# Transposing softmax probabilities as 4-byte words of two bf16 keys in a cached-attention kernel

## The chip, the cores and the metric

The kernel runs on one core of one Trainium2 chip. The metric is the device time of one execution in microseconds (us). Three runs of the kernel before took 1212.93, 1213.23 and 1215.47 us; the median is 1213.23 us. The five engines of the core that the text names are TensorE (PE in the profile, with PEld for its weight loads), VectorE (DVE), ScalarE (ACT), GpSimd (POOL) and SyncE (SP, which here only issues DMAs).

## The reference, cut to what matters

Two problems, A and B, of the same shape are computed one after the other and their outputs put side by side. All inputs are bf16.

```python
# per problem: B=16 batch elements, Sq=144 queries, D=448, H=16 heads, Sk=512 keys, Dh=256
q = (x @ wq).reshape(B, Sq, H, Dh).transpose(0, 2, 1, 3)
scores = jnp.einsum("bhqd,bhkd->bhqk", q, k_cache) * (Dh ** -0.5)
p = softmax(scores, axis=-1)
o = jnp.einsum("bhqk,bhkd->bhqd", p, v_cache)
out = o.transpose(0, 2, 1, 3).reshape(B, Sq, H * Dh) @ wo
# result: concatenate([out_A, out_B], axis=-1)
```

## The kernel before, in words

One head of one batch element is a *unit*; there are 512 units, 256 for each problem. Four consecutive units are a *group* (128 of them) and eight units are what one load of keys covers.

The 144 queries of a unit are split into 112 (part A, handled unit by unit) and 32 (part B, handled for four units together, so that they fill 128 partitions). For every unit the kernel does the following.

- Q (L314): eight matmuls of 144 columns project x onto the head and leave q transposed in PSUM. It is evacuated to `qt_sb` by VectorE (L326) or ScalarE (L330), scaled by 1/16.
- SA (L418): two matmuls of 512 columns give the scores of the 112 queries in one of the two banks `sa_ps`. VectorE takes the negated maximum (L429); ScalarE takes the exponential into `pa_sb` as bf16 and sums it (L440); VectorE inverts the sum (L450); GpSimd multiplies the row by it (L458).
- TA (L471): TensorE transposes the probabilities, in four transposes of 112 queries by 128 keys. The data are the weights of the matmul and the identity is the operand that streams. The keys of one transpose are every fourth key: `pa_sb` is read with a step of four elements, since the values lie in SBUF with four consecutive keys in one partition. The result goes as bf16 into the same bank of `sa_ps` that held the scores of this unit, and VectorE copies it to `pt_sb` (L481).
- PV (L504): eight matmuls of 144 columns, four chunks of keys for each half of the head dimension. The weights are the values and the streaming operand is P^T out of `pt_sb`. ScalarE evacuates the result to a ring buffer (L519, L521).
- OP (L542): output projection, pieces of two matmuls of 448 columns, as soon as 128 rows of a batch element's heads are complete. ScalarE evacuates it (L560), and GpSimd's queue stores it (L571).

Part B goes the same way for groups: SB (L342) makes the scores of eight units with 16 matmuls that use 32 columns of weights each, TB (L394) makes four transposes of 128 by 128 for a group, and VectorE copies them to the four `pt_sb` slots of the group (L403). The softmax steps are L354, L364, L374 and L382.

The order of the work is written out as one loop over i. In iteration i the kernel emits Q of unit i+15, SB once in eight iterations, SA of unit i+5, TA of unit i+2, TB for a group once in four iterations, PV of unit i, and pieces of OP. Each engine executes its own list in that order. A small planner (`_Sched`) adds the waits: an operation waits on the semaphore counters of those that wrote what it reads, or that still use a buffer or a PSUM bank that it writes. PSUM banks are the scarce buffers: `sa_ps` has two, so the transposes of unit u+2 go into a bank that the scores of unit u+4 have just left, which means after the maximum and the exponential of unit u+4. SP's queue carries the loads of x, wq, wo, K (with a transposing DMA, L290, three buffers of eight units) and V (L299, three buffers of four units), in the order of planned due times.

`S.add(engine, emit, reads, writes, banks)` below records one operation for the planner; `pta_ps` and `ptb_ps` are the banks of part A and B as the transposes see them, before the change the bf16 view of the fp32 banks.

Of the kernel before, what the change touches and what calls it, by code (L numbers as in the profile page):

```python
# [5 lines left out]
BF16 = mybir.dt.bfloat16  # L6
F32 = mybir.dt.float32
# [115 lines left out]
def bass_concat_heads__mha_block_cached__gqa_block_cached__near_ridge_kernel(  # L123
# [19 lines left out]
    Bn, SQ, D = A_x.shape  # L143
# [3 lines left out]
    QA, QB = 112, 32  # L147
# [17 lines left out]
    NQT, NPA, NPB, NPT, NST, NSTB, NOST = 12, 5, 2, 8, 4, 2, 3  # L165
# [9 lines left out]
    with contextlib.ExitStack() as es:  # L175
        def sb(name, shape, dt):
            return es.enter_context(nc.sbuf_tensor(name, shape, dt))

        def ps(name, shape, dt):
            return es.enter_context(nc.psum_tensor(name, shape, dt))  # L180
# [7 lines left out]
        qt_sb = sb("qt_sb", [128, NQT, 2, SQ], BF16)  # L188
        pa_sb = sb("pa_sb", [128, NPA, SK], BF16)
        pb_sb = sb("pb_sb", [128, NPB, SK], BF16)  # L190
        pt_sb = sb("pt_sb", [128, NPT, 4, SQ], BF16)
        ost_sb = sb("ost_sb", [128, NOST, D], BF16)
        ident = sb("ident", [128, 128], BF16)
        ones = sb("ones", [128, 128], BF16)
        stat = sb("stat", [128, 3 * NST + 3 * NSTB + 2], F32)
        qp_ps = ps("qp_ps", [128, 512], F32)
        sa_ps = [ps("sa_ps%d" % i, [128, 512], F32) for i in range(2)]
        sb_ps = [ps("sb_ps%d" % i, [128, 512], F32) for i in range(2)]
        ot_ps = [ps("ot_ps%d" % i, [128, 512], F32) for i in range(2)]
        op_ps = ps("op_ps", [128, 512], F32)  # L200
        pta_ps = [t.bitcast(BF16) for t in sa_ps]
        ptb_ps = [t.bitcast(BF16) for t in sb_ps]

        S = _Sched()
        sem_names = list(COMPUTE)
# [181 lines left out]
        def t_tb(G):  # L387
            psl = G % NPB

            def e(t):  # L390
                src = pb_sb[:, psl, :].rearrange("q (p c) -> q c p", c=4)
                ins = None
                for c in range(4):
                    ins = t.transpose(ptb_ps[G % 2][:, c * 128:(c + 1) * 128], src[:, c, :], ident[:, :])  # L394
                return ins
            S.add(PE, e, reads=[(("pb", psl), (G, 1)), ("ident", 0)], writes=[(("sbb", G % 2), ("t", G))],
                  banks=["sb%d" % (G % 2)], name="TB%d" % G)

        def t_evac_ptb(G):
            s0 = (4 * G) % NPT  # L400

            def e(v):
                return v.tensor_copy(pt_sb[:, s0:s0 + 4, :, QA:SQ],  # L403
                                     ptb_ps[G % 2][:, 0:512].rearrange("p (c j q) -> p j c q", c=4, j=4))
            S.add(DVE, e, reads=[(("sbb", G % 2), ("t", G))],
                  writes=[(("ptb", (4 * G + j) % NPT), 4 * G + j) for j in range(4)], banks=["sb%d" % (G % 2)],
                  name="eptb%d" % G)
# [55 lines left out]
        def t_ta(U):  # L463
            psl = U % NPA
            bank = U % 2

            def e(t):
                src = pa_sb[0:QA, psl, :].rearrange("q (p c) -> q c p", c=4)
                ins = None
                for c in range(4):  # L470
                    ins = t.transpose(pta_ps[bank][:, c * 128:c * 128 + QA], src[:, c, :], ident[0:QA, 0:QA])  # L471
                return ins
            S.add(PE, e, reads=[(("pa", psl), (U, 1)), ("ident", 0)], writes=[(("sap", bank), ("t", U))],
                  banks=["sa%d" % bank], name="TA%d" % U)

        def t_evac_pta(U):
            sl = U % NPT
            bank = U % 2

            def e(v):  # L480
                return v.tensor_copy(pt_sb[:, sl, :, 0:QA],  # L481
                                     pta_ps[bank][:, 0:512].rearrange("p (c q) -> p c q", c=4)[:, :, 0:QA])
            S.add(DVE, e, reads=[(("sap", bank), ("t", U))], writes=[(("pta", sl), U)], banks=["sa%d" % bank],
                  name="epta%d" % U)

# [8 lines left out]
        def t_pv(U):  # L494
            G, j = divmod(U, 4)
            vsl = G % NV
            sl = U % NPT
            ob = U % 2

            def e(t):  # L500
                ins = None
                for dc in range(2):
                    for c in range(4):
                        ins = t.matmul(ot_ps[ob][:, dc * SQ:(dc + 1) * SQ],  # L504
                                       lhsT=v_sb[:, vsl, j, c * DH + dc * 128:c * DH + (dc + 1) * 128],
                                       rhs=pt_sb[:, sl, c, :], start=(c == 0), stop=(c == 3))
                return ins
            S.add(PE, e, reads=[(("v", vsl), G), (("pta", sl), U), (("ptb", sl), U)], writes=[(("otp", ob), U)],
                  banks=["ot%d" % ob], name="PV%d" % U)
# [75 lines left out]
        for XG in range(NXGT):  # L585
            pr, j = divmod(XG, Bn // XB)
# [214 lines left out]
```

## Time and profile before

| what | value |
|---|---|
| median of the runs | 1213.23 us (1212.93 to 1215.47) |
| profiled execution, first to last instruction | 1210.9 us |
| TensorE busy | 1176.6 us (97%), 13952 matmuls and as many weight loads |
| VectorE, ScalarE, GpSimd busy | 770.1, 753.9 and 679.6 us |
| granted TensorE clock, mean | 0.997 |
| transposes L471, L394 | 2048 and 512 matmuls |
| PV matmuls L504 | 4096 |
| HBM read and written | 148.90 MB and 4.13 MB |

How to read it: the span goes from the first to the last instruction of the profiled execution. No time of its own is listed for that execution beside its span; the span lies 2.3 us under the median of the runs. "Busy" counts the time in which at least one instruction of the engine was running; a matmul's duration includes its latency, and consecutive matmuls overlap. The chain is the sequence of work that ended last, followed back from the last instruction; its pieces add up to the span. A group of instructions shows line, engine, operation, out<-in, shapes and count, then busy time and mean ns of one, then the idle time of the engine just before them and who ended it.

### The profile page before, as it was taken

The numbers are of one execution on the slowest core, as the hardware profiler recorded it, in microseconds if no ns is written. First come the engines' busy times: TensorE is split into PE (matmuls) and PEld (weight loads), VectorE is DVE, ScalarE is ACT, GpSimd is POOL, SyncE is SP. The second block draws the span as 40 slices with busy tenths as digits, with TensorE's granted clock in tenths as the row PEclk, the third lists the DMA queues.
The fourth block names the chain that finished last, engine by engine and source line by source line (L and its number), as shares of the span: only waits on it lengthen the run. The fifth ranks groups of instructions, "written<-read, shape, count | busy, mean of one in ns | idle before, by whom it ended". The sixth has DMA issues, their size and how long they took to land.

```text
span 1210.9 us, 33868 instructions
## 1 busy us (share of the span) xinstructions
PE 1176.6 (97%) x13952; PEld 902.6 (75%) x13952; DVE 770.1 (64%) x2179; ACT 753.9 (62%) x2213; POOL 679.6 (56%) x682
## 2 busy tenths in 40 slices
PE   4998999999999999999999999999999999999997
PEld 3676777777777777777777777777877777777765
DVE  1765666666666666666566666666666666666563
ACT  1655666666666666666566666666666666666553
POOL 0654565565555565565555655655655655655553
PEclk9999999999999999999999999999999999999999
DMA  9999999999999999999999999999999999999971
GB/s 250 296 269 290 246 255 225 242 251 246 245 238 234 228 263 231 239 239 233 278 284 272 278 272 267 247 257 224 245 245 236 226 245 244 244 239 243 223 178 47
DMA packets 627033, 294.15 MB, mean 243 GB/s; under 512 B 548416, under 2 KB 556608, under 8 KB 626880
## 3 DMA queue, kind: packets, MB, share of 16 engines
q1 hardware_dynamic: 625152, 287.85, 102.2%
q0 software_dynamic: 1728, 4.13, 1.2%
q8 instruction: 111, 1.82, 0.6%
q14 instruction: 42, 0.34, 0.1%
HBM read 148.90 MB, written 4.13 MB: 126 GB/s over the span
## 4 chain that ended last, share of the span: by engine, by line
PE 90%; DMA 6%; DVE 2%; SPq 1%; ACT 0%; issue 0%; POOL 0%; ACTq 0%
PE qp_ps L314 20%; PE ot_ps L504 19%; PE sa_ps L418 18%; PE op_ps L542 17%; PE sa_ps L471 8%; PE sb_ps L342 5%; DMA kt_sb<-in_A_k_cache_dram 4%; PE sb_ps L394 2%; DMA kt_sb<-in_B_k_cache_dram 1%; DVE stat L429 1%; DMA wq_sb<-in_A_wq_dram 0%; PE qp_ps L542 0%; SPq L280 0%; DVE qt_sb L326 0%; DVE pt_sb L481 0%
## 5 line engine op out<-in xcount | busy, mean ns | idle before, releaser
L458 POOL TENSOR_TENSOR pa_sb<-pa_sb,stat 112x512 bf16<-112x512 bf16 x512 | 532.7, 1041 | 491.6 <-DVE stat L450 491.4
L440 ACT ACTIVATE pa_sb<-sa_ps,stat 112x512 bf16<-112x512 f32 x512 | 352.0, 688 | 409.6 <-DVE stat L429 408.6
L429 DVE TENSOR_REDUCE stat<-sa_ps 112x1 f32<-112x512 f32 x512 | 353.9, 691 | 324.7 <-PE sa_ps L418 321.4
L314 PEld LDWEIGHTS qp_ps<-xt_sb,wq_sb 128*128 128x128 bf16 x4096 | 290.5, 99 | 93.1 <-issue 11.3
L314 PE MATMUL qp_ps<-xt_sb,wq_sb 128*128 128x144 bf16 x4096 | 344.1, 228 | 16.1 <-DMA wq_sb<-in_A_wq_dram 10.3
L504 PE MATMUL ot_ps<-pt_sb,v_sb 128*128 128x144 bf16 x4096 | 340.9, 226 | 0.0
L418 PE MATMUL sa_ps<-kt_sb,qt_sb 128*112 128x512 bf16 x1024 | 311.1, 385 | 1.0 <-DVE pt_sb L481 0.8
L542 PE MATMUL op_ps<-wo_sb,ring 128*128 128x448 bf16 x1120 | 279.6, 353 | 0.0
L504 PEld LDWEIGHTS ot_ps<-pt_sb,v_sb 128*128 128x128 bf16 x4096 | 269.1, 98 | 0.4
L471 PEld LDWEIGHTS sa_ps<-ident,pa_sb 112*128 112x128 bf16 x2048 | 161.2, 114 | 104.9 <-ACT pa_sb L440 24.8
L519 ACT ACTIVATE ring<-ot_ps 128x288 bf16<-128x288 f32 (+8 forms) x512 | 190.3, 372 | 4.5 <-PE ot_ps L504 4.5
L481 DVE COPY pt_sb<-sa_ps 128x448 bf16<-128x448 bf16 x512 | 190.5, 372 | 2.4 <-PE sa_ps L471 2.4
L471 PE MATMUL sa_ps<-ident,pa_sb 112*128 112x112 bf16 x2048 | 186.5, 213 | 0.1
L326 DVE TENSOR_SCALAR qt_sb<-qp_ps 128x288 bf16<-128x288 f32 x256 | 117.0, 457 | 98.2 <-PE qp_ps L314 97.5
L382 POOL TENSOR_TENSOR pb_sb<-pb_sb,stat 128x512 bf16<-128x512 bf16 x128 | 133.1, 1040 | 27.1 <-DVE stat L374 27.1
L330 ACT ACTIVATE qt_sb<-qp_ps 128x288 bf16<-128x288 f32 x256 | 106.0, 414 | 35.1 <-PE qp_ps L314 33.4
L418 PEld LDWEIGHTS sa_ps<-kt_sb,qt_sb 128*112 128x112 bf16 x1024 | 96.9, 129 | 38.5 <-issue 26.8
L542 PEld LDWEIGHTS op_ps<-wo_sb,ring 128*128 128x128 bf16 x1120 | 95.5, 98 | 28.1 <-issue 0.9
L440 ACT ACTIVATION_READ_ACCUMULATOR pa_sb<-sa_ps,stat 112x1 f32 x512 | 98.9, 193 | 0.0
L354 DVE TENSOR_REDUCE stat<-sb_ps 128x1 f32<-128x512 f32 x128 | 87.1, 680 | 3.6 <-PE sb_ps L342 3.6
L364 ACT ACTIVATE pb_sb<-sb_ps,stat 128x512 bf16<-128x512 f32 x128 | 88.5, 691 | 0.0
L450 DVE RECIPROCAL stat<-stat 112x1 f32<-112x1 f32 x512 | 78.4, 153 | 0.5 <-ACT pa_sb L440 0.5
(23 smaller groups left out, 368.4 us busy)
## 6 DMA issues: line engine op xcount, KB each, us to landing
v_sb<-in_A_v_cache_dram SPq DMA_DIRECT2D x64, 1024.0 KB, 6.0
v_sb<-in_B_v_cache_dram SPq DMA_DIRECT2D x64, 1024.0 KB, 6.1
out_dram<-ost_sb POOLq DMA_DIRECT2D x36, 112.0 KB, 5.1
wo_sb<-in_A_wo_dram SPq DMA_DIRECT2D x8, 448.0 KB, 7.4
wo_sb<-in_B_wo_dram SPq DMA_DIRECT2D x8, 448.0 KB, 5.7
wq_sb<-in_A_wq_dram SPq DMA_DIRECT2D x4, 768.0 KB, 6.2
wq_sb<-in_B_wq_dram SPq DMA_DIRECT2D x4, 768.0 KB, 7.8
wq_sb<-in_A_wq_dram SPq DMA_DIRECT2D x4, 128.0 KB, 6.6
```

What stands on the lines that cost most here:

```text
L314: ins = t.matmul(qp_ps[:, dc * SQ:(dc + 1) * SQ], lhsT=wq_sb[:, kc, c0:c0 + 128], rhs=xt_sb[:, xsl, kc, xo:xo + SQ], start=(kc == 0 and dc ...
L326: return v.tensor_scalar(qt_sb[:, sl, :, :], src, 1.0 / 16.0, None, op0=ALU.mult)
L382: return g.tensor_tensor(pb_sb[:, psl, :], pb_sb[:, psl, :], stat[:, RINVB + sl:RINVB + sl + 1].to_broadcast([128, SK]), op=ALU.mult)
L418: ins = t.matmul(sa_ps[bank][0:QA, :], lhsT=qt_sb[:, U % NQT, dc, 0:QA], rhs=kt_sb[:, ksl, dc, ko:ko + SK], start=(dc == 0), stop=(dc == 1))
L429: return v.tensor_reduce(stat[0:QA, NEG + sl:NEG + sl + 1], sa_ps[bank][0:QA, :], axis=AX.X, op=ALU.max, negate=True)
L440: return a.activation(pa_sb[0:QA, psl, :], sa_ps[bank][0:QA, :], AF.Exp, bias=stat[0:QA, NEG + sl:NEG + sl + 1], scale=1.0, accum_out=stat ...
L458: return g.tensor_tensor(pa_sb[0:QA, psl, :], pa_sb[0:QA, psl, :], stat[0:QA, RINV + sl:RINV + sl + 1].to_broadcast([QA, SK]), op=ALU.mult)
L471: ins = t.transpose(pta_ps[bank][:, c * 128:c * 128 + QA], src[:, c, :], ident[0:QA, 0:QA])
L481: return v.tensor_copy(pt_sb[:, sl, :, 0:QA], pta_ps[bank][:, 0:512].rearrange("p (c q) -> p c q", c=4)[:, :, 0:QA])
L504: ins = t.matmul(ot_ps[ob][:, dc * SQ:(dc + 1) * SQ], lhsT=v_sb[:, vsl, j, c * DH + dc * 128:c * DH + (dc + 1) * 128], rhs=pt_sb[:, sl, c, ...
L519: ins = a.activation(ring[:, 2 * h:2 * h + 2, c0:c0 + n1], src[:, :, 0:n1], AF.Copy)
L542: ins = t.matmul(acc[0:m, 0:D], lhsT=ring[:, c, col0:col0 + m], rhs=wo_sb[:, c, :], start=(c == first), stop=(c == last))
```

## The change

The probabilities of a row are viewed as 32-bit words, each with two neighbouring bf16 keys, and the words are transposed as 4-byte numbers. A transpose then moves 256 keys instead of 128, so TA and TB have two transposes in place of four, which read words with a step of two. The identity becomes fp32. In PSUM a transposed word lies in one fp32 column, with the two keys beside each other; VectorE copies the same number of bf16 elements as before to `pt_sb`, in which query and key pair are now the two inner dimensions. The streaming operand of PV takes one key of each pair and so steps by two elements. The waits, the banks, the sizes of the buffers and the order of the work stay as they are.

```diff
-        pt_sb = sb("pt_sb", [128, NPT, 4, SQ], BF16)
+        pt_sb = sb("pt_sb", [128, NPT, 2, SQ, 2], BF16)
...
-        ident = sb("ident", [128, 128], BF16)
-        ones = sb("ones", [128, 128], BF16)
+        ident = sb("ident", [128, 128], F32)
+        ones = sb("ones", [128, 128], F32)
...
-        pta_ps = [t.bitcast(BF16) for t in sa_ps]
-        ptb_ps = [t.bitcast(BF16) for t in sb_ps]
+        pta_ps = sa_ps
+        ptb_ps = sb_ps
+        pta_h = [t.bitcast(BF16) for t in sa_ps]
+        ptb_h = [t.bitcast(BF16) for t in sb_ps]
+        pa_w = pa_sb.bitcast(F32)
+        pb_w = pb_sb.bitcast(F32)
...
# t_tb
-                src = pb_sb[:, psl, :].rearrange("q (p c) -> q c p", c=4)
+                src = pb_w[:, psl, :].rearrange("q (p c) -> q c p", c=2)
                 ins = None
-                for c in range(4):
+                for c in range(2):
                     ins = t.transpose(ptb_ps[G % 2][:, c * 128:(c + 1) * 128], src[:, c, :], ident[:, :])
# t_evac_ptb
-                return v.tensor_copy(pt_sb[:, s0:s0 + 4, :, QA:SQ],
-                                     ptb_ps[G % 2][:, 0:512].rearrange("p (c j q) -> p j c q", c=4, j=4))
+                return v.tensor_copy(pt_sb[:, s0:s0 + 4, :, QA:SQ, :].rearrange("p j c q e -> p j c (q e)"),
+                                     ptb_h[G % 2][:, 0:512].rearrange("p (c j q) -> p j c q", c=2, j=4))
# t_ta
-                src = pa_sb[0:QA, psl, :].rearrange("q (p c) -> q c p", c=4)
+                src = pa_w[0:QA, psl, :].rearrange("q (p c) -> q c p", c=2)
                 ins = None
-                for c in range(4):
+                for c in range(2):
                     ins = t.transpose(pta_ps[bank][:, c * 128:c * 128 + QA], src[:, c, :], ident[0:QA, 0:QA])
# t_evac_pta
-                return v.tensor_copy(pt_sb[:, sl, :, 0:QA],
-                                     pta_ps[bank][:, 0:512].rearrange("p (c q) -> p c q", c=4)[:, :, 0:QA])
+                return v.tensor_copy(pt_sb[:, sl, :, 0:QA, :].rearrange("p c q e -> p c (q e)"),
+                                     pta_h[bank][:, 0:512].rearrange("p (c q) -> p c q", c=2)[:, :, 0:2 * QA])
# t_pv
-                                       rhs=pt_sb[:, sl, c, :], start=(c == 0), stop=(c == 3))
+                                       rhs=pt_sb[:, sl, c // 2, :, c % 2], start=(c == 0), stop=(c == 3))
```

## The prediction

> **What bounds the kernel now.** I began with the page: busy time, the chain that ended last, and the lines of the operations that the diff touches.
>
> ```profile
> span 1210.9 us, 33868 instructions
> PE 1176.6 (97%) x13952; PEld 902.6 (75%) x13952; DVE 770.1 (64%) x2179; ACT 753.9 (62%) x2213; POOL 679.6 (56%) x682
> ...
> PE 90%; DMA 6%; DVE 2%; SPq 1%; ACT 0%; issue 0%; POOL 0%; ACTq 0%
> PE qp_ps L314 20%; PE ot_ps L504 19%; PE sa_ps L418 18%; PE op_ps L542 17%; PE sa_ps L471 8%; PE sb_ps L342 5%; DMA kt_sb<-in_A_k_cache_dram 4%; PE sb_ps L394 2%; DMA kt_sb<-in_B_k_cache_dram 1%; DVE stat L429 1%; DMA wq_sb<-in_A_wq_dram 0%; PE qp_ps L542 0%; SPq L280 0%; DVE qt_sb L326 0%; DVE pt_sb L481 0%
> ```
>
> TensorE is busy 97% of the span and owns 90% of the chain; VectorE and ScalarE are a third idle. Whatever leaves or enters TensorE's stream moves the end. Busy time counts each matmul with its latency, so the price of a matmul has to be read elsewhere: the chain in order of time, between 500 and 513 us, gives each group's own share (start, length, group).
>
> ```profile
> 503.41 0.43 PE sa_ps L418 x2
> 503.85 0.20 PE sa_ps L471 x4
> 504.04 0.50 PE ot_ps L504 x8
> 504.55 0.38 PE op_ps L542 x2
> 504.92 0.50 PE qp_ps L314 x8
> ...
> 509.88 0.20 PE sa_ps L471 x4
> 510.08 0.23 PE sb_ps L394 x4
> ```
>
> A unit (one head of one batch element) takes 2.01 us here. Four transposes L471 cost 0.20 us (49 ns each), four L394, once in four units, 0.23 us (56 ns each), eight PV matmuls L504 0.50 us (62.8 ns each). The 49 ns are 112 columns at the 0.416 ns per column of L418 (0.43 us for 1024 columns) and some 2 ns; the 62.8 ns are 144 columns likewise. So a matmul costs its columns, and its weight load is hidden under the one before it.
>
> The loads, from the groups of the load queue by form (mean ns behind the bar):
>
> ```profile
> L504 PEld LDWEIGHTS ot_ps<-pt_sb,v_sb 128*128 128x128 bf16 x4096 | 269.1, 98 | 0.4
> L471 PEld LDWEIGHTS sa_ps<-ident,pa_sb 112*128 112x128 bf16 x2048 | 161.2, 114 | 104.9 <-ACT pa_sb L440 24.8 <-issue 0.3
> L418 PEld LDWEIGHTS sa_ps<-kt_sb,qt_sb 128*112 128x112 bf16 x1024 | 96.9, 129 | 38.5 <-issue 26.8 <-DVE pt_sb L481 1.9
> L342 PEld LDWEIGHTS sb_ps<-kt_sb,qt_sb 128*32 128x32 bf16 x1024 | 21.9, 96 | 33.5 <-issue 10.4 <-DVE pt_sb L403 3.8 <-ACT qt_sb L330 0.8
> ```
>
> L418 and L342 differ by 80 columns and 33 ns: 0.41 ns per column on a fixed 83 ns. Over those 83, L504 takes 15 ns and L471, which reads with a step of four elements, 31 ns: here the step doubles the reading time. And L471 is the one load that waits, for the exponential on ScalarE.
>
> **The change part by part.**
>
> *Transposes.* 512 groups of four become two, 128 groups likewise: 1024 + 256 matmuls and as many loads go, and the remaining ones handle 4-byte words. No row shows TensorE with 4-byte operands, so this price is bounded. Low end: a word column streams like a bf16 column (49 and 56 ns) and its load reads 128 words at L418's rate, 53 ns. Two groups back to back then cost, for TA alone, 55 (second transpose, held by its load and 2 ns) + 49 = 0.104 us against 0.20; for TA and TB together, where three loads follow short transposes, 3 x 55 + 56 = 0.221 against 0.43. Saved: 384 x 0.096 + 128 x 0.209 = 37 + 27 = 64 us. Upper end of a load in one pass: L418's rate doubled as L471's is by its step, 109 ns; then 111 + 49 = 0.160 and 3 x 111 + 56 = 0.389, and 384 x 0.040 + 128 x 0.041 = 21 us are saved. Upper end of all: each word column goes through twice, each time behind a 109 ns load: 4 x 111 = 0.444 us a group, and (0.444 - 0.20) x 512 + (0.444 - 0.23) x 128 = 152 us are lost. I take the low end. A word load puts 512 bytes per partition into 53 ns (9.7 per ns); L471's strided load already brings 256 bytes in 31 ns (8.3 per ns) through the same step of eight bytes, so that row is near the low end; and the streamed identity is contiguous like every streamed operand here.
>
> The Trainium skill speaks on both sides, and no run here shows either. "TensorE: Matmul & The Clock Gate", Terms, says that transpose mode is four times faster for FP32, which against the four passes that "FP8 and Floating Point Precision" gives true FP32 is one pass, my low end; its section on weight-path modes turns the fast load off for FP32, and its LDWEIGHTS section has 1/1.2 ns per column, an estimated 107 ns for 128, where L418 and L342 show half of that per column. Without the transpose mode four passes would make 8 x 49 ns a group, an estimated loss of (0.392 - 0.20) x 512 + (0.448 - 0.23) x 128 = 126 us.
>
> *PV's streamed operand.* The 4096 matmuls of L504 read P^T with a step of two elements. No streamed operand has a step now. Low end: nothing. Upper end: what the step of four does to L471's load, 31 against 15 ns, applied to 60 ns of streaming: 62.8 becomes 125.8, and 4096 x 63 = +258 us. I take nothing: half the step of L471, one element at a time where the load fetches 128 columns in 15 ns, so the row that doubles is a far quicker reader than this one has to be. It stays the dearest doubt.
>
> "SBUF — State Buffer", A bandwidth-pool intuition that's wrong (the note on cachelines), wants two hits per 16-byte line for full rate: a step of two bf16 has four and would be free, but so would L471's step of four with its two, and the trace shows 16 ns for it, so I don't lean on the rule.
>
> *Evacuations.* L481 and L403 copy as many bf16 elements from as many partitions (372 and 414 ns now) in longer runs. Costed at nothing: VectorE is 64% busy. If the new pattern cost 100 ns more, 640 x 0.1 = 64 us of VectorE would raise it to 69%, and PV, which reads the result two units later, would not see it. The 4-byte identity on GpSimd (0.3 + 0.2 us at the start) lies under the wait of 10.3 us for wq.
>
> *What is late next.* Scores of unit u+4 and transposes of unit u+2 share a bank, so the transposes' load waits for max and exponential of the later scores:
>
> ```profile
> PEld sa_ps L471 <- ACT pa_sb L440: 24.8, 88, 0.6
> ```
>
> From the first score matmul 0.63 us pass to the max, then 0.69 + 0.03 + 0.69 + 0.19, then 0.05 to the load: 2.29 us, spread over two units. With P the length of a unit and O its output projection, 2P is at least 2.35 + transposes 0.20 + PV 0.50 + Q 0.50 + O, so P is at least 1.78 + O/2, against 1.63 + O unhindered. With 0.10 for the transposes: 1.73 + O/2 against 1.53 + O. The 88 units that wait already keep 0.05 of 0.10 us (4 us lost); the most frequent kind (O = 0.38; 222 of 512 by the chain's pieces) stands at 1.92 against 1.91, and the longer load adds some 0.01: 4 us. Behind the waiting load stand PV and Q on the same queue, which is why the whole unit slips.
>
> *DMA.* Keys are queued behind values on SP, whose own waits give it air:
>
> ```profile
> SPq L299 <- PE op_ps L542: 235.3, 59, 12.8
> ```
>
> That is 235.3 / 64 = 3.7 us of idle queue per key load of eight units, while units shorter by 0.1 us take 0.8 us of it away. The page's throughput, some 240 GB/s in the middle slices, reaches 290 in the first slices. Only the start and the change to problem B, where weights come too and TensorE waits for keys now (7.9 + 0.8 us), gain nothing: some 50 units x 0.12 = 6 us.
>
> Sum: -64 + 4 + 4 + 6 = -50 us on the profiled span of 1210.9. The span lies 2.3 us under the median of the runs, 1213.2, which carries the same launch work: 1213 - 50 = 1163 us.
>
> **The rivals.**
> 1. *The step costs PV its rate* (slower than before). At L504; for it the doubled load at L471, against it the smaller step and the slower reader. Price 258 us: 1163 + 258 = 1421 us, 1400 to 1440 by the transposes' share. It decides the sign from 50 / 4096 = 12 ns per PV matmul on.
> 2. *A word is worth more than two bf16 columns.* For it: twice the bytes per column in load and stream, nothing in the trace that shows them at one pass. Twice through with 53 ns loads is 4 x 55 = 0.22 us a group, 512 x 0.02 = +10, 1223 us; with 109 ns loads 1213 + 152 = 1365; in the middle 1295 us.
> 3. *The step costs a part.* Step four doubles; of its three extra elements step two has one: a third of 63 ns, 21 x 4096 = +86 us, 1249 us. Nothing in the trace shows a part; a range of 1190 to 1270.
> 4. That the change saves nothing because another engine is next is weak: only the 8 us of the exponential's loop speak for it.
>
> **How the numbers follow.** Forecast 0.42 (0.40 faster, 0.01 same, 0.01 slower): 1163, own range 1149 to 1205 (64 saved with no loss; 21 saved less 13). Rival 1 0.28, all slower. Rival 2 0.20 (0.01, 0.01, 0.18). Rival 3 0.10 (0.01, 0.01, 0.08). Faster 0.42, same 0.03, slower 0.55: the likeliest single case is faster, yet more of the chance lies with the two unseen prices. The range goes from 1149 to 1425: all but the dearer half of rival 1 is inside. Within 0.2% (2.4 us, the spread of the three runs) counts as the same.
>
> **What the next profile would show.** Matmul counts of 12672; L471's group at 0.10 us and TA with TB at 0.22 in the chain; L504 still at 0.50 for eight; the wait of L471 for L440 in many more than 88 units; L418 and L314 unchanged. Wrong if eight PV matmuls take about a microsecond (rival 1), 0.67 (rival 3), or if two word transposes take 0.2 us or more (rival 2), in stream or in loads that no longer start ahead.

## The result, and the profile after

The changed kernel takes 1229.5 us (median of four runs, 1228.23 to 1230.46) against 1214.3 us for the kernel before in the same comparison: a ratio of 1.0125, 95% interval 1.0108 to 1.0141. It is 1.25% slower. The point forecast, 1163 us, is wrong by 66 us and in direction; slower had been given a chance of 0.55.

The page of the kernel after has the counts that were expected and a TensorE that is as full as before:

```profile
span 1227.9 us, 31308 instructions
PE 1195.0 (97%) x12672; PEld 961.9 (78%) x12672; DVE 772.8 (63%) x2179; ACT 754.0 (61%) x2213; POOL 678.9 (55%) x682
...
PE 91%; DMA 6%; SPq 1%; DVE 1%; ACT 0%; issue 0%; POOL 0%; ACTq 0%
```

1280 matmuls went and TensorE's busy time rose by 18 us, that of its weight loads by 59. No other engine moved by more than 3 us, and TensorE still owns the chain. (All lines of the kernel moved down by four or so: L471 is now L475, L394 L398, L504 L508, L418 L422.) The chain in order of time has the same groups as those shown of before:

```profile
504.04 0.43 PE sa_ps L422 x2
504.48 0.22 PE sa_ps L475 x2
504.69 0.52 PE ot_ps L508 x8
...
506.52 0.21 PE sa_ps L475 x2
506.73 0.25 PE sb_ps L398 x2
506.99 0.51 PE ot_ps L508 x8
```

Two word transposes take 0.21 to 0.22 us where four bf16 ones took 0.20; two of TB take 0.25 us against 0.23; eight PV matmuls take 0.51 to 0.52 against 0.50. Two word transposes at 0.2 us or more are the sign that the prediction named for rival 2. The load queue shows the rows that the prediction had to bound (mean ns behind the bar):

```profile
L475 PEld LDWEIGHTS sa_ps<-ident,pa_sb 112*128 112x128 f32 x1024 | 193.8, 197 | 68.1 <-ACT pa_sb L444 23.2
L398 PEld LDWEIGHTS sb_ps<-ident,pb_sb 128*128 128x128 f32 x256 | 43.2, 217 | 0.1
```

Over the fixed 83 ns a word load takes 114 ns for TA and 134 for TB, not 53. The full account comes from the trace: the time from each matmul's start to the start of the next, added up by the group of the first one. These times cover the span from the first to the last matmul.

| group | before, us | after, us | difference |
|---|---|---|---|
| transposes TA | 102.7 | 116.1 | +13.4 |
| transposes TB | 29.4 | 33.1 | +3.7 |
| PV | 258.2 | 267.0 | +8.8 |
| Q | 292.3 | 285.9 | -6.4 |
| SA, SB, OP | 511.1 | 508.3 | -2.8 |
| sum | 1193.7 | 1210.3 | +16.6 |

The span grew by 17.0 us. So the change costs 26 us in the groups that it touches, and 9 us come back elsewhere: matmuls behind Q and the others wait less when a unit is longer. Per matmul, the second TA transpose starts 100 ns after the first (medians), PV starts 113 ns after the second, TB has 134 and 121 ns, and PV matmuls follow each other at 64 to 65 ns instead of 62 to 63.

### The profile page after: what moved, and what is told of

Same layout as the page of the kernel before. It is cut to its first block, busy times and chain, and to the rows that moved or that the text cites. A ratio compares the mean times of both kernels' runs of the same rounds, so it can differ in the third digit from the quotient of the medians.

```text
span 1227.9 us, 31308 instructions
## 1 busy us (share of the span) xinstructions
PE 1195.0 (97%) x12672; PEld 961.9 (78%) x12672; DVE 772.8 (63%) x2179; ACT 754.0 (61%) x2213; POOL 678.9 (55%) x682
## 4 chain that ended last, share of the span: by engine, by line
PE 91%; DMA 6%; SPq 1%; DVE 1%; ACT 0%; issue 0%; POOL 0%; ACTq 0%
PE ot_ps L508 20%; PE qp_ps L318 20%; PE sa_ps L422 18%; PE op_ps L546 16%; PE sa_ps L475 9%; PE sb_ps L346 5%; DMA kt_sb<-in_A_k_cache_dram 4%; PE sb_ps L398 2%; DMA kt_sb<-in_B_k_cache_dram 1%; DMA wq_sb<-in_A_wq_dram 1%; PE qp_ps L546 0%; SPq L285 0%; SPq L284 0%; DVE stat L433 0%; DVE qt_sb L330 0%
## 5 line engine op out<-in xcount | busy, mean ns | idle before, releaser
L508 PE MATMUL ot_ps<-pt_sb,v_sb 128*128 128x144 bf16 x4096 | 348.9, 226 | 0.0
L422 PE MATMUL sa_ps<-kt_sb,qt_sb 128*112 128x512 bf16 x1024 | 310.1, 384 | 0.6 <-DVE pt_sb L485 0.6
L508 PEld LDWEIGHTS ot_ps<-pt_sb,v_sb 128*128 128x128 bf16 x4096 | 306.9, 98 | 1.8
L475 PEld LDWEIGHTS sa_ps<-ident,pa_sb 112*128 112x128 f32 x1024 | 193.8, 197 | 68.1 <-ACT pa_sb L444 23.2
L475 PE MATMUL sa_ps<-ident,pa_sb 112*128 112x112 f32 x1024 | 199.7, 276 | 0.1
L485 DVE COPY pt_sb<-sa_ps 128x448 bf16<-128x448 bf16 x512 | 190.4, 372 | 2.6 <-PE sa_ps L475 2.6
L422 PEld LDWEIGHTS sa_ps<-kt_sb,qt_sb 128*112 128x112 bf16 x1024 | 97.1, 129 | 33.5 <-issue 26.8
```

The lines of the kernel that those rows point to most:

```text
L422: ins = t.matmul(sa_ps[bank][0:QA, :], lhsT=qt_sb[:, U % NQT, dc, 0:QA], rhs=kt_sb[:, ksl, dc, ko:ko + SK], start=(dc == 0), stop=(dc == 1))
L485: return v.tensor_copy(pt_sb[:, sl, :, 0:QA, :].rearrange("p c q e -> p c (q e)"), pta_h[bank][:, 0:512].rearrange("p (c q) -> p c q", c=2 ...
L508: ins = t.matmul(ot_ps[ob][:, dc * SQ:(dc + 1) * SQ], lhsT=v_sb[:, vsl, j, c * DH + dc * 128:c * DH + (dc + 1) * 128], rhs=pt_sb[:, sl, c ...
```

## The experiments

Where a kernel pairs keys with other values or leaves work out, its expectation says which part. Ratios are to the kernel before.

**1. PV's step alone.** The transposes stay bf16; PV reads the same bytes of the buffer through a view with a step of two.

```diff
+        pt_v = pt_sb.rearrange("p s (c e) q -> p s c (e q)", e=2).rearrange("p s c (q e) -> p s c q e", e=2)
...
-                                       rhs=pt_sb[:, sl, c, :], start=(c == 0), stop=(c == 3))
+                                       rhs=pt_v[:, sl, c // 2, :, c % 2], start=(c == 0), stop=(c == 3))
```

> The kernel before with one edit: PV reads its streamed operand with a step of two inside the same buffer (it pairs keys and queries wrongly, so only its time counts). Step theory: the step itself costs each PV matmul some 2 ns (64 to 65 ns from one to the next against 62.8), 4096 x 2.1 = +9 us, about 1223 us, transposes unchanged at 0.20 us. Rival (PV is slower after the change only because it follows the word transposes): PV stays at 62.8 ns and the time at 1214 us.

Measured: 1220.6 us, ratio 1.0052 (1.0032 to 1.0072). PV's sum rises from 258.2 to 268.0 us, each matmul at 64 to 65 ns, and the transposes stay at 102.5 and 29.4 us. The step itself is the cause: it costs 2.4 ns a matmul, 10 us of TensorE, of which 4 us are covered by shorter waits. The time comes out 2 us below the expected one. The chain shows the price beside unchanged transposes:

```profile
400.64 0.20 PE sa_ps L473 x4
400.84 0.52 PE ot_ps L506 x8
```

**2. The words alone.** The changed kernel, with PV reading flat.

```diff
+        pt_v = pt_sb.rearrange("p s c q e -> p s c (q e)").rearrange("p s c (e q) -> p s c e q", e=2)
...
-                                       rhs=pt_sb[:, sl, c // 2, :, c % 2], start=(c == 0), stop=(c == 3))
+                                       rhs=pt_v[:, sl, c // 2, c % 2, :], start=(c == 0), stop=(c == 3))
```

> The changed kernel with one edit: PV reads the same buffer without a step (again keys and queries are paired wrongly, only the time counts). Step theory: about 1229.5 - 9 = 1220.5 us, PV back at 62.8 ns, transposes as in the changed kernel (100 and 113 ns for TA, 134 and 120 for TB). Rival: 1229 us, PV stays at 64 to 65 ns.

Measured: 1224.5 us, ratio 1.0080 (1.0061 to 1.0100). PV is back at 257.7 us; the transposes keep 116.4 and 33.0 us. The time is 4 us above the expected one, which took off the whole 9 us of PV's step although only a part of it shows in the time. The prices of runs 1 and 2 are separate; since waits cover a part of each, their times (+6.2 and +10.1 us) add up to 16.3 against the 15.2 us of the whole change.

**3. Words side by side.** Is it the stepped load that makes the word transposes slow?

```diff
-                src = pa_w[0:QA, psl, :].rearrange("q (p c) -> q c p", c=2)
+                src = pa_w[0:QA, psl, :].rearrange("q (c p) -> q c p", c=2)
# the same in t_tb
```

> The changed kernel with the words of one transpose taken side by side instead of every second one, so that the weight load reads without a step; values are left in their order, so each key meets another key's value and only the time counts. Theory A (the transposes are slow because the load of stepped words is slow): the load of 195 ns falls to some 137, and the matmuls come after 55 to 60 ns instead of 100 to 134: some 1024 x 50 + 256 x 68 = 68 us less, about 1165 us. Theory B (a word streams through TensorE at the time of two bf16 columns, whatever the load does): 100 and 113 ns stay, 1229 us, even if the load gets shorter.

Measured: 1218.3 us, ratio 1.0036 (1.0023 to 1.0049). Neither theory had it whole. The load does what theory A said,

```profile
L475 PEld LDWEIGHTS sa_ps<-ident,pa_sb 112*128 112x128 f32 x1024 | 138.0, 142 | 93.1 <-ACT pa_sb L444 24.7 <-issue 0.4
L398 PEld LDWEIGHTS sb_ps<-ident,pb_sb 128*128 128x128 f32 x256 | 30.3, 140 | 0.2
```

142 ns instead of 197, which is 59 over the fixed 83. But the matmuls hardly follow: in the chain of this run the groups are back at the time of the kernel before, and no lower.

```profile
401.36 0.19 PE sa_ps L475 x2
401.55 0.22 PE sb_ps L398 x2
401.77 0.52 PE ot_ps L508 x8
```

TA takes 100 + 95 ns, TB 113 + 108. The sums are 102.7 and 28.8 us against 102.7 and 29.4 before: half as many transposes in the same time. The stepped load explains the 17 us by which the changed kernel's transposes are dearer than bf16 ones; it does not explain why the 64 us never came. That is theory B's part, and runs 5 to 8 test it.

**4. What two transposes less would have been worth.** Half of the bf16 transposes are left out.

```diff
-                for c in range(4):
+                for c in range(2):
                     ins = t.transpose(...)   # in t_ta and t_tb; the evacuations copy two chunks
```

> The kernel before with two of the four transposes left out in TA and TB: half of the keys is never transposed (the buffer holds zeros there), VectorE copies half as much, all else is there. It shows what two transposes a unit at the price of bf16 ones would have been worth. The prediction's sum: 64 us leave TensorE, 8 us come back as waits for the exponential and 6 at the keys' loads: about 1163 us. Rival (the loop over max and exponential or the loads of keys take most of it): 1190 us or more, with the wait of the transposes' load for ScalarE far above 25 us or waits for keys far above 9 us.

Measured: 1161.1 us, ratio 0.9567 (0.9543 to 0.9591). TA and TB fall to 54.5 and 15.3 us, 62 us less. The waits that the prediction saw coming are there:

```profile
PEld sa_ps L476 <- ACT pa_sb L445: 34.8, 88, 0.7
PE sb_ps L347 <- DMA kt_sb<-in_A_k_cache_dram: 10.5, 7, 3.0
PE sb_ps L347 <- DMA kt_sb<-in_B_k_cache_dram: 2.5, 2, 2.3
```

The transposes' load waits 35 us for ScalarE against 25, and keys are waited for 13 us against 9. By the trace, the load starts 51 ns after the exponential of the later unit ends in 310 units, against 88 before, which is the spread to many more units that the prediction expected; in most of them the short bf16 load still hides under the score matmul, and the wait view lists 88 both times. TensorE's sum falls by 53.8 us, so 8.5 of the 62 us are lost where the prediction had 14. Its sum thus holds to 3 us (53 us measured, 50 forecast) once a transpose costs what a bf16 one does. Two things are kinder here than in the forecast: the loads are those of bf16, and VectorE copies half as much.

**5 and 6. Half of the streamed columns.** If a word column streams at 0.83 ns, 56 queries instead of 112 should halve a transpose.

```diff
-                src = pa_w[0:QA, psl, :].rearrange(...)
+                src = pa_w[0:QH, psl, :].rearrange(...)          # QH = 56, words side by side (5) or stepped (6)
... # the copy to pt_sb is cut likewise
-                    ins = t.transpose(pta_ps[bank][:, c * 128:c * 128 + QA], src[:, c, :], ident[0:QA, 0:QA])
+                    ins = t.transpose(pta_ps[bank][:, c * 128:c * 128 + QH], src[:, c, :], ident[0:QH, 0:QH])
```

> The run with the words of a transpose side by side, with only the first 56 of the 112 queries transposed in TA (56 partitions, identity of 56 columns; the other queries of part A stay zero and VectorE copies half as much). Theory B (a word column streams at twice a bf16 column, 0.83 ns): each TA transpose falls from 95 to 100 ns to 47 + 2, at most to some 60 if its load of 142 ns then leads. Theory C (a 4-byte transpose has a fixed price that the number of columns doesn't move): 95 to 100 ns stay.

> The changed kernel with the same cut to 56 queries in TA, the words still read with a step of two. If the stepped load (196 ns, 113 of them above the fixed 83) is what holds the second transpose, the two transposes together stay near 2 x 110 minus the part of the stream that lies behind the load, 165 us at the least of the 213 ns of the changed kernel. If the load is no limit, they fall to some 100 to 110 ns like the run with the words side by side.

Measured: 1290.6 and 1352.0 us, one run each, both far slower than with 112 queries, and no answer to the question. The load queue of run 5 shows why:

```profile
506.06 0.20 PEld L481 LDWEIGHTS sa_ps<-ident,pa_sb 56*128 56x128 f32 x2 [0.39 <-ACT ring L529]
506.32 0.25 PEld L514 LDWEIGHTS ot_ps<-pt_sb,v_sb 128*128 128x128 bf16 x4
```

In the trace the second score matmul of this unit starts at 505.76, and its 512 columns take 0.216 us; the transpose's load starts at 506.06, 0.31 us after it, where with 112 queries it starts 2 ns after it. The view puts the idle time down to ScalarE (L529), but the delay is 307 or 308 ns in nearly all of the 512 units, and a wait for another engine would vary. The matmuls behind are late by as much: the medians are 310 ns from the last score matmul to the transpose against 216, and 154 ns from the transposes to PV against 95. With 56 partitions the load no longer runs ahead of a matmul of 128 partitions, nor PV's load ahead of these transposes. The cut was repeated with 72 partitions.

**7 and 8. The same with 72 queries.**

```diff
-    QH = 56
+    QH = 72
```

> The words of a transpose side by side, and 72 of the 112 queries transposed in TA (more than 64 partitions, so that the load should start under the last score matmul again, which it did not with 56; the other 40 queries of part A stay zero). Theory B (a word column takes 0.83 ns to stream): 72 x 0.83 + 2 = 62 ns for each of the two transposes instead of 95 to 100, at most some 70 if a load of 142 ns leads; two transposes 125 to 140 ns against 200. Theory C (a fixed price of a 4-byte transpose): 95 to 100 ns each.

> The changed kernel with the same cut to 72 queries, words read with a step of two. If the second stepped load (196 ns) holds the second transpose, the two take about as long as in the changed kernel less a part of their stream: 165 to 210 ns together; if only the streams count, 125 to 140 ns.

Measured: 1191.8 and 1218.2 us, one run each. With the words side by side,

```profile
L481 PEld LDWEIGHTS sa_ps<-ident,pa_sb 72*128 72x128 f32 x1024 | 137.7, 141 | 100.3 <-ACT pa_sb L450 31.1 <-issue 0.8
```

the load runs ahead again and keeps its length, and the group shrinks:

```profile
402.28 0.43 PE sa_ps L428 x2
402.71 0.13 PE sa_ps L481 x2
402.83 0.52 PE ot_ps L514 x8
```

The transposes take 67 + 62 ns against 100 + 95. Forty columns less are 33 ns less: 0.83 ns for a word column, twice the 0.42 of a bf16 column, with 2 ns on top; TB's 108 ns for 128 columns lie on the same line. Theory B is shown; the fixed price of theory C is out. (Columns and partitions were cut together. For bf16 it is the columns that count: on 128 partitions 512 columns take 216 ns and 144 take 62.) With stepped words the first transpose falls to 67 ns as well, but PV still starts 113 ns after the second one, as with 112 queries:

```profile
404.50 0.18 PE sa_ps L481 x2
404.68 0.52 PE ot_ps L514 x8
```

That 113 ns is, to 1 ns, what the stepped load takes over the fixed 83 (197 less 83). In the trace the first load starts 214 ns before its transpose, with the score matmul; the second starts 1 ns after the first transpose and has only that one to hide under. Where TB follows TA, the four transposes take 466 ns with 72 queries and 467 with 112 (medians, to the start of PV); with words side by side it is 349 against 416. So with the step it is the loads that set the time of all but the first transpose, and without it the columns.

**9. Steps of one to four in PV.** How far is a stepped stream from being free?

```diff
+        pt_f = pt_sb.rearrange("p s c q -> p s (c q)")
...
-                                       rhs=pt_sb[:, sl, c, :], start=(c == 0), stop=(c == 3))
+                                       rhs=pt_f[:, sl, 0:SQ * (c + 1):c + 1], start=(c == 0), stop=(c == 3))
```

> The kernel before with PV's four key chunks read from the same buffer with steps of one, two, three and four elements in turn (keys and queries paired wrongly, only the time counts). If the streamed operand behaves like the weight load of L471 (twice the time at a step of four): 62.5, 64.5, about 95 and 126 ns from one matmul to the next, some 1024 x 95 = +97 us in all, 1310 us. If a step costs a fixed 2 ns: 62.5 and three times 64.5, 1221 us.

Measured: 1298.0 us, one run. In the first four matmuls of a unit the next one starts, by mean, after 65.6 ns (step one, 65.7 before), 64.7 (two), 92.5 (three) and 115.3 ns (four). The fifth matmul, with step one again, keeps the next one waiting for 83.3 ns instead of 62.6, so a step of four costs some 136 ns in all. PV's sum is 355.2 us, 97.0 more than before; the time rises by 84 us, as 14 us go from the times behind Q's matmuls. The first theory is right in kind: a step of four doubles the stream, as it doubles L471's load, while a step of two is nearly free.

**10. Both reads flat.** The changes of runs 2 and 3 together.

> The changed kernel with both reads without a step: the words of a transpose side by side and PV's operand flat (keys and values paired wrongly, only the time counts). What is left of the change is two word transposes in place of four bf16 ones. If the three prices add up (stream even, stepped load +17 us of TensorE, PV's step +9 us): TensorE's groups as before, 0.195 us for TA, and the time of the kernel before within 3 us, about 1214 us. If the words have a price of their own beyond these: 1220 us or more; if a gain is hidden behind the two steps: 1205 us or less.

Measured: 1212.4 us, ratio 0.9981 (0.9967 to 0.9995). TensorE's sum is 1193.6 us against 1193.7 before, TA 102.7 against 102.7, PV 257.2 against 258.2, and the profiled span is 1210.9 us for both:

```profile
401.54 0.20 PE sa_ps L477 x2
401.74 0.22 PE sb_ps L400 x2
401.96 0.50 PE ot_ps L510 x8
```

The median is 2 us lower, and the interval just leaves out equality. What is left of the change without its two steps is worth nothing that these sums show, and no version that beats the kernel before by a clear margin is in sight on this way: with these pairings a correct kernel would also need another order of the values and a stepped copy on VectorE (by the code; not run).

## Why the prediction was right or wrong

- *The sum.* Forecast: -64 us for the transposes, nothing for PV, +14 for waits, together -50. Measured in TensorE's account: +17, +9 and -9, together +17.
- *What bounds the kernel.* Right. TensorE's stream sets the end before and after, and run 4 turns 62 us taken from it into 53 us of time. That a load hides under the matmul before it does not hold for the stepped word load.
- *Transposes.* Wrong, and this step decides the result. The prediction took the low end of its bound: "a word column streams like a bf16 column (49 and 56 ns)". It streams in 0.83 ns, twice as long (runs 3 and 7), so two word transposes cost what four bf16 ones did, and the 64 us were never there. The reason given for the low end looked at bytes per ns of the load and at a contiguous identity; neither says how long TensorE takes for a 4-byte column. Rival 2 had this price, at its low end of 1223 us, but was quoted at a middle of 1295; its picture, each word column going through twice behind a load of its own, is not what the trace shows, which has one load for each transpose (12672 of each) and a slower stream.
- *The load of words.* Wrong in size: 53 ns taken, 114 (TA) and 134 (TB) measured with the step, where 109 was the upper end of a load in one pass, and 59 without. That L471's rate "is near the low end" was the wrong row to lean on; the step doubled this load too. Cost: 17 us, the whole surplus of TA and TB over bf16.
- *PV's stream.* Costed at nothing, with 258 us as the upper end and 86 us in between. It is 2.4 ns a matmul, 10 us (run 1). That it came out so small was in part luck. One of the two reasons, that the stream is a slower reader than L471's load and so stands a step better, fails in run 9: at the load's own step of four the stream doubles too (62.8 to some 136 ns). The other reason, half the step, is left, and at a step of three the stream already takes 1.5 times as long. Rivals 1 and 3 did not happen.
- *Evacuations.* Right: L485 and L407 take 372 and 415 ns as before.
- *What is late next, and DMA.* Right in mechanism and, at 8.5 us against 14, in order of size, though the change never called them up: run 4 shows both waits. In the changed kernel the opposite happens, units get longer and 9 us of waits go. The prediction did not count that a loss, too, is partly covered.
- *The chances.* Slower held 0.55, but 0.36 of it stood on rivals 1 and 3 and the rest almost wholly on rival 2 with its middle of 1295 us. That the larger chance lay on the side that came true is therefore largely luck.
- *The skill's rules.* The factor of four for FP32 in transpose mode, in the Trainium skill's "TensorE: Matmul & The Clock Gate", Terms, does not mean the rate of bf16 here: the runs show half of it per column, whatever the factor is counted from. The P/1.2 ns for a load of P columns in its section "LDWEIGHTS (loading the stationary operand)", an estimated 107 ns for 128, is near the 114 of the stepped load and far from the 59 of the flat one. The two hits per line of "SBUF — State Buffer" (the note on cachelines, in the section on Door 1) are contradicted for the stream by run 9: a step of four bf16 has two and costs some 136 ns instead of 62 to 65.

## What to carry to other kernels

Packing two narrow values into a wider word saves instructions, not TensorE time, if the engine streams the wide word at half the rate: count columns times time per column of that type, and while no row shows that type, give the doubled rate at least the weight of the single one. Look at every read whose step or element size changes as a price of its own; here each was small beside the gain hoped for, and they were all that was left when the gain proved to be none. An experiment that leaves out the work which a change means to save tells its worth before the change is written: run 4 gave 53 us for half of the transposes.

## What the runs showed of the hardware that was not expected

- A 4-byte transpose streams a column in 0.83 ns, against 0.42 for bf16, while PV's streamed operand with a step of two sweeps the same four bytes per column in 0.45 ns. So it is not the bytes that the stream passes over. Nor is it the width of the output alone: the score matmuls write fp32 columns at 0.42 ns each. Data and identity became 4 bytes wide together, and which of them takes the second 0.42 ns was not settled.
- A weight load with 56 partitions starts 307 ns after the start of the 512-column matmul of 128 partitions before it, whose columns take 216; with 72 partitions it starts under it (2 to 15 ns after its start, medians of runs 8 and 7). The transpose follows the score matmul after 310 ns instead of 216, and run 5 is 72 us slower than run 3 although it transposes half of part A's queries. Where between 56 and 72 this changes, and why, was not measured.
- A streamed bf16 operand of 144 columns takes 65, 92 and some 136 ns with a step of two, three and four, against 62 to 63 without a step; of the 136, 21 show only behind the matmul that follows.
